# Attention with an MLP on one core: a hand-written opening, and q and k turned on VectorE from the seventh group on

## The chip, the cores and the metric

The kernel runs on one core of a Trainium2 chip. The metric is the device time of one execution in microseconds, lower is better; a run's time is that of its slowest core, and here there is only one.

## The reference

q, k and v have the shape (8, 12, 448, 64) in float32: 8 batches, 12 heads, 448 tokens, 64 features a head. Each row of q and k is normalised by its root mean square and multiplied by a gain; then comes attention, then a two-layer MLP over all 3584 tokens with 768 features, 2048 hidden units, and a slope alpha for each hidden unit where the hidden value is negative.

```python
def rmsnorm(x, g):
    rms = np.sqrt(np.mean(x * x, axis=-1, keepdims=True) + 1e-06)
    return x / rms * g
q_n, k_n = (rmsnorm(q, g_q), rmsnorm(k, g_k))
scores = scale * np.matmul(q_n, k_n.transpose(0, 1, 3, 2))
attn = softmax(scores)                      # written out in the reference
x = (attn @ v).transpose(0, 2, 1, 3).reshape(3584, 768)

h = x @ w_in                                # 768 x 2048
g = np.maximum(h, 0.0) + alpha * np.minimum(h, 0.0)
out = g @ w_out                             # 2048 x 768, float32
```

## The kernel before

**Groups, tiles, bursts.** The heads are taken in groups of four, three groups a batch, 24 groups in all, numbered y = 0 to 23 (`G = 3`, `NG = 24`). The 448 keys of a group are seven tiles of 64 (`J = 7`); a score tile is written (y, j). The whole run is a list of 69 bursts, written out by hand. A burst holds some score tiles, and behind them `gaps[n]`: steps of the MLP (`up`, `down` and, late in the run, the `quad` steps, which replace down steps by fewer products of mixed weights). Dictionaries say in which burst a group's factors are computed (`roots`), where its q and k are made ready (`turn_at`), where loads stand (`nexts`) and where softmax denominators and the product with v stand (`dens`, `avs`). `jobs[n]` holds small pieces that are put behind single steps of burst n, one after each `up`, and later in the run after every second one. The order of each engine's instructions is the order in which this code issues them.

**From q and k to their turned form.** For each group `load_qk` (L126) loads q and k in their natural layout, tokens on the partitions, by SP's queue. `square` (L177) squares them, mostly on GpSimd; `reduce` (L185, VectorE) sums the squares; `root` (L195, L196, ScalarE) takes the power -1/2 by Ln and Exp; `scale` (L205) multiplies q and k by it into the f16 tile `qs`, for the first groups on VectorE, later on GpSimd. Then q and k are turned, so that features lie on the partitions. For the first seven groups, `TD = 7`, TensorE does it: 14 transposes (L330) into PSUM, which VectorE evicts to `qT` (L337) and `kT` (L339, with the gain). From y = 7 on, `turn_dma` (L304) issues two DMA transposes on SP's queue right behind the scale, and some bursts later `turn` multiplies k by the gain in place on VectorE (L315, in the form that also writes an accumulator):

```python
if y >= TD:
    t = qkT[y, "k"].rearrange("p j g c -> p (j g c)")
    nc.vector.tensor_scalar(
        out=t, in0=t, scalar1=gain[:, 0:1], scalar2=None, op0=ALU.mult,
        op1=ALU.max, accum_out=mark32,
    )
```

**Attention and MLP.** `score` (L357, TensorE) makes a score tile in PSUM (tag "sc", two tiles of two banks) and `soft` (L371, ScalarE) takes its exponential to `expT`. `den` and `attv` (L382, TensorE) sum over keys, with ones and with v; `log` and `invert` (ScalarE) give the reciprocal, and VectorE writes x of the batch (L464, L481). An `up` step is six products of `w_in` and x into a bank `hT` of tag "mm" (L496; some use a spare bank, `hTa`); ScalarE writes the part scaled by alpha (L536), and VectorE combines both into `gT` (L540), which frees the bank. `down` (L558) multiplies by `w_out`, VectorE evicts (L569), and SP's queue stores (L546). The quads add products (L623), sums on VectorE and GpSimd (L611, L612, L619), mixed weights on GpSimd (L591), and evictions with sums (L681, L686).

**The opening.** The first eleven bursts (0 to 10) go through the same loop, with special cases: q and k of group 0 are taken in parts (`part_square` L171, `part_reduce`, `part_root`, `part_scale` L245, `part_turn` L256, `part_copy` L266 and L272), group 1 is turned by `turn_one`, and one burst, `lead`, has an order of its own. The gains and alpha come by GpSimd loads into one tile, which one transpose turns to columns (L995). `spin` issues products without a use, which keep TensorE busy. `follow` (L279) is a one-column copy on GpSimd that makes its queue wait for a scale.

Of the kernel before, what the change touches and what calls it, by code (L numbers as in the profile page):

```python
# [21 lines left out]
def kernel(  # L22
# [26 lines left out]
    TD = min(7, NG)  # L49
# [31 lines left out]
    cols = cst.tile([128, NF + 2], FP32, name="cols", tag="cols")  # L81
    alpha_sb = cols[:, :NF]
# [24 lines left out]
    SRC = {"q": q4, "k": k4}  # L107


    rows = lent(0, 512)[: NF + 2]  # L110

    def load_qk(y, hold=False):
        b, i = divmod(y, G)
        for nm in "qk":
            if y in (2, 5, 8):
                t = lent(HB + "qk".index(nm) * NB4, NB4).rearrange(
                    "p (h j d) -> p h j d", h=2, j=J
                )
            else:
                t = ld.tile([128, 2, J, D], FP32, name="nat", tag="nat", bufs=4)  # L120
            if hold and nm == "q":

                nc.scalar.copy(out=t[:, 0, 0, 0:1], in_=expb)
            o = t.rearrange("p h j d -> p h (j d)")
            for h in range(2) if (y, nm) == (0, "q") else (slice(0, 2),):
                nc.sync.dma_start(out=o[:, h], in_=SRC[nm][b, :, ds(2 * i, 2)][:, h])  # L126
            nat[y, nm] = t
# [9 lines left out]
    def load_w_in(c):  # L137

        src = moe_w_in[:512].rearrange("(n x p) f -> n p x f", n=4, p=32)
        for n in range(4):  # L140
            nc.gpsimd.dma_start(
                out=w_in_sb[ds(32 * n, 32), :4, ts(c, FB)], in_=src[n, :, :, ts(c, FB)]
            )
        if c % 2 == 0:
# [18 lines left out]
    def square(y, nm):  # L163
# [6 lines left out]
        if (y, nm) == (1, "q"):  # L170
            nc.scalar.activation(out=sqf, in_=src, func=AF.Square)  # L171
        else:

            n = 2 if (y, nm) in ((2, "q"), (G, "k")) else 1
            for h in range(n):
                c = ts(h, 2 * J * D // n)
                nc.gpsimd.tensor_mul(out=sqf[:, c], in0=src[:, c], in1=src[:, c])  # L177
# [20 lines left out]
    def scale(y, nm):  # L198
        if y in (1, 3, 5):
            t = lent(HB + 4 * NB4 + "qk".index(nm) * NB4 // 2, NB4 // 2).bitcast(FP16)  # L200
            t = t.rearrange("p (j h d) -> p j h d", j=J, h=2)
        else:
            t = ld.tile([128, J, 2, D], FP16, name="qs", tag="qs", bufs=2)
        eng = nc.vector if y < G or (y, nm) == (G, "q") else nc.gpsimd
        eng.tensor_mul(  # L205
            out=t.rearrange("p j h d -> p h j d"),
            in0=nat[y, nm],
            in1=rr_t[y][:, "qk".index(nm)].unsqueeze(3).broadcast_to((128, 2, J, D)),
# [33 lines left out]
    def part_scale(nm, j, n, eng):  # L242
        if (0, nm) not in qs:
            qs[0, nm] = ld.tile([128, J, 2, D], FP16, name="qs", tag="qs", bufs=2)
        eng.tensor_mul(  # L245
            out=qs[0, nm][:, j].rearrange("p j h d -> p h j d"),
            in0=nat[0, nm][:, :, j],
            in1=rr_t[0][:, "qk".index(nm), :, j].unsqueeze(3).broadcast_to((128, 2, n, D)),
# [11 lines left out]
    def part_copy(nm, j, eng):  # L260
# [4 lines left out]
        if nm == "k":  # L265
            nc.vector.tensor_scalar(  # L266
                out=o, in0=tp, scalar1=gain[:, 0:1], scalar2=None, op0=ALU.mult
            )
        elif eng is nc.scalar:
            nc.scalar.copy(out=o, in_=tp)  # L270
        else:
            eng.tensor_copy(out=o, in_=tp)  # L272
# [4 lines left out]
    def follow(y, nm):  # L277

        nc.gpsimd.tensor_copy(out=mark, in_=qs[y, nm][:, J - 1, 1, D - 1 : D])  # L279

    def turn_one(y, nm):
        t = psf.tile([128, 512], FP32, name="tps", tag="mm")
        tp = t[:, :S].bitcast(FP16).rearrange("p (j c) -> p j c", j=J)
        for j in range(J):
# [3 lines left out]
        t = att.tile([128, J, 2, 64], FP16, name=f"{nm}T", tag=f"{nm}T", bufs=3)  # L288
        o = t.rearrange("p j g c -> p j (g c)")
        if nm == "q":  # L290
            nc.vector.tensor_copy(out=o, in_=tp)
        else:

            for c in (slice(0, 2), slice(2, J)):
                nc.vector.tensor_scalar(
                    out=o[:, c], in0=tp[:, c], scalar1=gain[:, 0:1], scalar2=None,
                    op0=ALU.mult,
                )
        qkT[y, nm] = t

    def turn_dma(y):
        for nm in "qk":
            t = att.tile([128, J, 2, 64], FP16, name=f"{nm}T", tag=f"{nm}T", bufs=3)
            nc.sync.dma_start(  # L304
                out=t.rearrange("p j g c -> p j (g c)"),
                in_=qs[y, nm].rearrange("p j h d -> p (j h d)"),
                transpose=True,
            )
            qkT[y, nm] = t

    def turn(y):

        if y >= TD:
            t = qkT[y, "k"].rearrange("p j g c -> p (j g c)")
# [5 lines left out]
        if y <= G:  # L320
            ps = [psf.tile([128, 512], FP32, name="tps", tag="mm") for _ in "qk"]
        else:
            ps2 = psa.tile([128, 2, 512], FP32, name="tps2", tag="acc")
# [26 lines left out]
    def score(y, j):  # L350
        qT, kT = qkT[y, "q"], qkT[y, "k"]
        sc = pss.tile([128, 2, 512], FP32, name="sc", tag="sc")
        m = 64 if y < EARLY else 32
        for c in range(64 // m):
            for par in range(2):
                for g in range(2):
# [4 lines left out]
                        lhsT=kT[ds(64 * par, 64), j, g, ts(c, m)],  # L361
                        rhs=qT[ds(64 * par, 64), :, g, :],
# [13 lines left out]
    def over_keys(accs, ys, weights):  # L376

        heads = [(y, par, c) for y in ys for c in range(3 - len(ys)) for par in range(2)]
        for j in range(J):
# [17 lines left out]
    def ones_over(accs, ys):  # L397

        if not halved(ys):
            return over_keys(accs, ys, lambda g, y, par, c, j: ones[ds(64 * g, 64)])  # L400
# [13 lines left out]
    def den(ys):  # L414
        dn = psa.tile([128, 2, 512], FP32, name="dn", tag="acc")
        ones_over((dn[:, 0], dn[:, 1]), ys)
        rden[ys] = dn
# [23 lines left out]
    def attv(ys, half, spare=False, jobs=(), put=None, early=False):  # L441

        b, i = divmod(ys[0], G)
# [5 lines left out]

        if half:  # L450
            av, accs = None, [psf.tile([128, 512], FP32, name="avb", tag="mm") for _ in range(2)]
        else:
            pool, tag = (pss, "sc") if spare else (psa, "acc")
            av = pool.tile([128, 2, 512], FP32, name="av", tag=tag)
            accs = (av[:, 0], av[:, 1])
        over_keys(accs, ys, weights)
        for f in jobs:
            f(ys)
        if b not in xT:
            xT[b] = att.tile([128, 2, G, S], FP16, name="xT", tag="xT")  # L460
# [31 lines left out]
    def up_part(hT, b, ft, lo, hi):  # L492

        for i in range(lo, hi):
            for g in range(2):
# [4 lines left out]
                    start=(i == 0 and g == 0),  # L500
                    stop=(i == G - 1 and g == 1),
                )

    def begin(ft):

        if ft < 2:
            begun[ft] = bank("hT", False)
        elif ft == 2:
            t = psa.tile([128, 2, 512], FP32, name="hTb", tag="acc")
            begun[2], begun[3] = t[:, 0], t[:, 1]  # L510
        up_part(begun[ft], 0, ft, 0, G - 1)
# [3 lines left out]
    def up(b, ft, spare=False):  # L515
        if b == 0 and ft in begun:
            hT = begun[ft]

            for n in {2: (2, 3), 3: ()}.get(ft, (ft,)):
                up_part(begun[n], 0, n, G - 1, G)  # L520
        else:
            hT = bank("hT", spare)
            up_part(hT, b, ft, 0, G)
# [300 lines left out]
    turn_at[2], turn_at[G] = 5, av_at[0]  # L824
    turn_at.update(
# [157 lines left out]
    nc.gpsimd.dma_start(out=rows[:NF], in_=moe_alpha.rearrange("(t p) -> t p", p=128))  # L983
    for n, g in enumerate((g_q, g_k)):
        for h in range(2):
            nc.gpsimd.dma_start(
                out=rows[NF + n : NF + n + 1, ds(64 * h, 64)], in_=g.unsqueeze(0)
            )
    load_qk(1, True)
    load_qk(2)  # L990

    spin(2)
    spin(17, False)
    ct = psf.tile([128, 512], FP32, name="ct", tag="mm")
    nc.tensor.transpose(ct[:, : NF + 2], rows, ident32[: NF + 2, : NF + 2])  # L995
    K0 = 3
    both, full, lo, hi = slice(0, 2), slice(0, J), slice(0, K0), slice(K0, J)
    for h in range(2):
        part_square("q", slice(h, h + 1), full, nc.scalar)
    for h in range(2):  # L1000
        part_reduce("q", slice(h, h + 1), full)
    part_root("q", full)
    part_scale("q", full, J, nc.gpsimd)
    part_square("k", both, lo, nc.scalar)
    part_square("k", both, hi, nc.scalar)
    part_reduce("k", both, lo)
    part_reduce("k", both, hi)
    part_root("k", lo)
    part_scale("k", lo, K0, nc.vector)
    part_root("k", hi)  # L1010
    square(1, "q")
    nc.vector.tensor_copy(out=cols, in_=ct[:, : NF + 2])
    nc.vector.tensor_mul(
        out=gain, in0=cols[:, NF : NF + 1], in1=cols[:, NF + 1 : NF + 2]
    )
# [3 lines left out]
    part_copy("k", lo, nc.vector)  # L1019
    load_v(0)  # L1020
    part_scale("k", hi, J - K0, nc.vector)
    follow(0, "k")
    square(1, "k")
    reduce(1, "q")
    square(2, "q")
    after(0, part_turn, "k", range(K0, J))
    after(0, part_copy, "k", hi, nc.vector)
    after(0, reduce, 1, "k")
    after(0, reduce, 2, "q", (0,))
    mid[1] = 1  # L1030
    after(1, square, 2, "k")
    after(1, load_w_in, 0)
    after(3, reduce, 2, "q", (1,))
    after(3, reduce, 2, "k")
    after(5, load_w_in, 1)
    after(7, load_w_in, 2)
    after(8, load_w_in, 3)
    for c in range(4):
        after(first + (0, 0, 3, 4)[c], load_w_out, c)
    for nm in "qk":  # L1040
        after(first, square, 2 * G, nm)
    mid[4] = 2

    since = 2
    for n in range(NB):
# [4 lines left out]
        lead = n == den_at[G - 1]  # L1050
        first_tiles = tiles[: 2 if lead else split.get(n, 2)]
        for t in first_tiles:
            if t == (0, J - 2):
                spin(1)
            elif t == (1, J - 3):
                spin(2, False)
            elif t == (1, J - 2):
                spin(1, False)
            elif t == (0, J - 1):
                turn_one(1, "q")  # L1060
            elif t == (1, 0):
                turn_one(1, "k")
# [167 lines left out]
```

## Time and profile before

| | |
|---|---|
| median of three runs | 413.3 us (412.49, 413.3, 414.25) |
| the profiled execution, its own time | 414.78 us |
| its span in the profile | 413.0 us |
| mean granted TensorE clock | 0.995 |
| TensorE busy | 398.9 us, 97% |
| VectorE, ScalarE, GpSimd busy | 65%, 62%, 62% |
| data moved | 53.38 MB, 129 GB/s on the mean |

The span runs from the first to the last instruction of the profiled execution; the device time lies 1.8 us above it. "PE" is TensorE's products, "PEld" its loads of weights, "DVE" is VectorE, "ACT" ScalarE, "POOL" GpSimd, "SP" the engine that issues most DMAs. A row of groups tells line, engine, operation, output and input tile, shape, count; then busy time, mean duration in ns; then the idle time of the engine ahead of them and what ended it. A row of the timeline tells start, duration and instruction, with the idle time ahead of it in brackets.

### The profile page before, as it was taken

How to read it: one execution, taken by the hardware profiler on the slowest of the kernel's cores; microseconds unless marked ns; L12 is line 12 of the kernel's file. 1: busy time of each engine (PE TensorE's matmuls, PEld its weight loads, DVE VectorE, ACT ScalarE, POOL GpSimd, SP SyncE). 2: the span in 40 equal slices, each digit the busy share in tenths (PEclk: the TensorE clock that was granted, in tenths of full speed). 3: DMA queues.
4: the chain of work that ended last, by engine and by line, in shares of the span. 5: the costliest groups of instructions: out<-in, count | busy, mean ns of one | idle time of the engine just before them, and what ended most of it. 6: DMA issues, size and time to landing. Idle time of an engine off the chain costs nothing.

```text
span 413.0 us, 11724 instructions
## 1 busy us (share of the span) xinstructions
PE 398.9 (97%) x5055; PEld 208.1 (50%) x5055; DVE 266.9 (65%) x420; ACT 257.3 (62%) x390; POOL 255.8 (62%) x184
## 2 busy tenths in 40 slices
PE   7889999899999999999999999999999999999996
PEld 3344445444456445554455445545555455645664
DVE  3876875476567388785688585958576755465322
ACT  5697787567846785557766786875657783135110
POOL 5599996589677969376373847484724407300870
PEclk9899999999999999999999999999999999999999
DMA  8999899957754894329861697279332700320143
GB/s 259 231 217 206 172 200 155 248 169 103 163 81 134 204 169 91 115 63 197 144 168 48 173 138 177 63 180 193 59 75 54 127 3 24 75 59 0 30 103 97
DMA packets 67330, 53.38 MB, mean 129 GB/s; under 512 B 34880, under 2 KB 66768, under 8 KB 67280
## 3 DMA queue, kind: packets, MB, share of 16 engines
q1 hardware_dynamic: 53344, 40.45, 40.5%
q0 software_dynamic: 13536, 11.81, 21.5%
q8 instruction: 39, 0.64, 0.7%
q10 hardware_dynamic: 400, 0.39, 0.3%
q14 instruction: 11, 0.09, 0.1%
HBM read 45.62 MB, written 11.01 MB: 137 GB/s over the span
## 4 chain that ended last, share of the span: by engine, by line
PE 49%; DVE 6%; ACT 0%; issue 0%; DVEq 0%
PE hT L496 14%; PE hTa L496 7%; PE qx L623 5%; PE sc L357 3%; PE oq L623 3%; PE qc L623 3%; PE qz L623 2%; PE av L382 2%; PE oqm L623 2%; PE avb L382 1%; PE dn L382 1%; PE oqa L623 1%; DVE ss L185 1%; DVE xT L481 1%; DVE kT L315 1%; PE qza L623 1%
## 5 line engine op out<-in xcount | busy, mean ns | idle before, releaser
L371 ACT ACTIVATE expT<-sc 128x896 f16<-128x896 f32 x168 | 147.8, 913 | 55.4 <-PE sc L357 55.0
L496 PE MATMUL hT<-xT,w_in_sb 128*128 128x448 f16 x546 | 113.7, 353 | 0.4 <-DVE gT L540 0.2
L496 PEld LDWEIGHTS <-w_in_sb 128*128 128x128 f16 x768 | 72.7, 98 | 74.8 <-issue 10.1
L540 DVE TENSOR_TENSOR gT<-hT,gT 128x448 f16<-128x448 f32 x91 | 56.6, 623 | 40.1 <-ACT gT L536 39.2
L205 POOL TENSOR_TENSOR qs<-nat,rr 128x896 f16<-128x896 f32 x36 | 60.9, 1713 | 33.4 <-issue 24.9
L536 ACT ACTIVATE gT<-hT,cols 128x448 f16<-128x448 f32 x90 | 56.9, 633 | 33.9 <-PE hT L496 33.7
L177 POOL TENSOR_TENSOR sq<-nat 128x896 f32<-128x896 f32 x32 | 53.1, 1681 | 38.0 <-DMA nat<-in_q_dram 25.3
L357 PE MATMUL sc<-qT,kT 64*32 64x448 f16 (+1 forms) x1092 | 53.3, 358 | 3.5 <-ACT expT L371 1.1
L623 PEld LDWEIGHTS <-gT 128*128 128x128 f16 x352 | 33.4, 98 | 26.0 <-issue 4.9
L496 PE MATMUL hTa<-xT,w_in_sb 128*128 128x448 f16 x210 | 45.4, 352 | 0.0
L185 DVE TENSOR_REDUCE ss<-sq 128x14 f32<-128x896 f32 (+1 forms) x37 | 38.3, 1052 | 0.6 <-POOL sq L177 0.6
L481 DVE TENSOR_TENSOR xT<-av,rden 64x448 f16<-64x448 f32 (+1 forms) x37 | 27.2, 734 | 13.5 <-PE av L382 5.5
L536 ACT ACTIVATE gT<-hTa,cols 128x448 f16<-128x448 f32 x35 | 22.2, 635 | 19.1 <-PE hTa L496 19.1
L540 DVE TENSOR_TENSOR gT<-hTa,gT 128x448 f16<-128x448 f32 x35 | 21.8, 624 | 17.7 <-ACT gT L536 17.6
L357 PEld LDWEIGHTS <-kT 64*32 64x32 f16 (+1 forms) x1092 | 15.6, 93 | 34.7 <-issue 29.3
L558 PE MATMUL op<-w_out_sb,gT 128*128 128x384 f16 x160 | 27.4, 326 | 0.0
L382 PEld LDWEIGHTS <-vt 64*32 64x32 f16 x1344 | 20.2, 92 | 14.1 <-issue 5.0
L611 POOL TENSOR_TENSOR gs<-gT 128x1024 f16<-128x1024 f16 x3 | 6.4, 2121 | 30.3 <-DVE gT L540 28.1
L558 PEld LDWEIGHTS <-gT 128*128 128x128 f16 x192 | 18.0, 98 | 13.5 <-issue 2.4
L382 PE MATMUL av<-expT,vt 64*32 64x448 f16 x896 | 24.3, 350 | 0.3 <-DVE osb L671 0.3
L619 POOL TENSOR_TENSOR gT<-gT 128x1024 f16<-128x1024 f16 x11 | 23.8, 2166 | 0.0
L623 PE MATMUL qx<-w_out_sb,gT 128*128 128x384 f16 x120 | 20.9, 326 | 0.0
(148 smaller groups left out, 494.1 us busy)
## 6 DMA issues: line engine op xcount, KB each, us to landing
out_dram<-osb SPq DMA_DIRECT2D x107, 96.0 KB, 2.8
nat<-in_k_dram SPq DMA_DIRECT2D x21, 448.0 KB, 5.4
nat<-in_q_dram SPq DMA_DIRECT2D x20, 448.0 KB, 4.9
vt<-in_v_dram POOLq DMA_DIRECT2D x8, 672.0 KB, 11.0
w_in_sb<-in_moe_w_in_dram POOLq DMA_DIRECT2D x24, 128.0 KB, 5.0
w_out_sb<-in_moe_w_out_dram POOLq DMA_DIRECT2D x4, 768.0 KB, 10.8
arena<-in_q_dram SPq DMA_DIRECT2D x3, 448.0 KB, 7.8
arena<-in_k_dram SPq DMA_DIRECT2D x3, 448.0 KB, 8.5
```

The source lines that it names most:

```text
L177: nc.gpsimd.tensor_mul(out=sqf[:, c], in0=src[:, c], in1=src[:, c])
L185: nc.vector.tensor_reduce(out=o[:, c], in_=sqs[y, nm][:, c], axis=AXIS_X, op=ALU.add)
L205: eng.tensor_mul(out=t.rearrange("p j h d -> p h j d"), in0=nat[y, nm], in1=rr_t[y][:, "qk".index(nm)].unsqueeze(3).broadcast_to((128, 2, ...
L357: nc.tensor.matmul(out=sc[ds(64 * g + m * c, m), par, :S].rearrange("p (j c) -> p j c", j=J), lhsT=kT[ds(64 * par, 64), j, g, ts(c, m)], r ...
L371: nc.scalar.activation(out=expT[y][:, j], in_=scs[y, j][:, :, :S], func=AF.Exp, scale=QK_SCALE, bias=EXP_BIAS,)
L382: nc.tensor.matmul(out=accs[g][ds(32 * n, 32), :S], lhsT=weights(g, y, par, c, j), rhs=expT[y][ds(64 * g, 64), j, par, :], start=(j == 0), ...
L481: nc.vector.tensor_mul(out=x, in0=av, in1=r)
L496: nc.tensor.matmul(out=hT[:, :S], lhsT=w_in_sb[:, block_of(g, i), ts(ft, 128)], rhs=xT[b][:, g, i, :], start=(i == 0 and g == 0), stop=(i ...
L536: nc.scalar.activation(out=g, in_=hT[:, :S], func=AF.Copy, scale=alpha_sb[:, ft : ft + 1])
L540: nc.vector.tensor_max(out=g, in0=hT[:, :S], in1=g)
L558: nc.tensor.matmul(out=op[:, :OH], lhsT=gT[:, ft, ts(tile % J, 128)], rhs=w_out_sb[:, ft, ts(oh, OH)], start=(ft == 0), stop=(ft == NF - 1),)
L623: nc.tensor.matmul(out=bank[:, c], lhsT=g[:, ft], rhs=v[:, ft, c], start=(first and ft == 0), stop=(ft == HF - 1), skip_group_check=True,)
```

## The change

It has two parts.

The opening is written out. The loop begins at burst 11 (`first + 1`), and everything before it stands as a list of calls. In it k of group 0 is loaded in halves on ScalarE's queue beside q on SP's; the load of q of group 1 is held until the first half of q(0) is there; the two gains come by two SP loads and are multiplied before they are turned, and alpha is turned by itself, later; the squares of group 0 are all on ScalarE; q(0) is scaled on VectorE and part of k(0) on GpSimd; the turned first part of k(0) is copied by ScalarE; the loads of v and `w_in` are issued in pieces at other places; the sums over keys for groups 0 to 2 are split and placed between score tiles, and the first `up` steps are begun in thirds; group 3 is turned in a bank of tag "sc", behind the third part of x.

From y = 6 on (`TD = 6`: 18 groups, one more than before left TensorE) q and k are turned otherwise. They are loaded with 14 neighbouring rows of 64 values to a partition (`FLAT`, 3584 bytes in one piece instead of 1792). `scale` writes straight into `qT` and `kT`, the two halves of a partition's rows interleaved value by value. `flip` transposes 32 x 32 blocks of 32-bit words into a tile of `qs` on VectorE, copies it back on VectorE, and moves four quarter blocks of 32 partitions by DMA on SP's queue. The two flips of a group are jobs of the burst behind the one with its root. `turn` applies the gain at its place as before. `score` takes its operands by other indices, with unchanged products.

```diff
-    TD = min(7, NG)
+    TD = 2 * G
...
+            if y >= TD:
+                nc.sync.dma_start(
+                    out=t.rearrange("p h j d -> p (h j d)"), in_=FLAT[nm][b, i]
+                )
+                continue
...
+            for h in range(2) if y == 0 else (slice(0, 2),):
+                (nc.scalar if (y, nm) == (0, "k") else nc.sync).dma_start(
+                    out=o[:, h], in_=SRC[nm][b, :, ds(2 * i, 2)][:, h]
+                )
...
+        if y >= TD:
+            o = t.rearrange("p b j c -> p (b j c)").rearrange(
+                "p (j d h) -> p h j d", j=J, h=2
+            )
...
-    def turn_dma(y):
-        for nm in "qk":
-            t = att.tile([128, J, 2, 64], FP16, name=f"{nm}T", tag=f"{nm}T", bufs=3)
-            nc.sync.dma_start(
-                out=t.rearrange("p j g c -> p j (g c)"),
-                in_=qs[y, nm].rearrange("p j h d -> p (j h d)"),
-                transpose=True,
-            )
-            qkT[y, nm] = t
+    def flip(y, nm):
+
+        t = qkT[y, nm].rearrange("p b j c -> p (b j c)")
+        x = ld.tile([128, J, 2, D], FP16, name="qs", tag="qs", bufs=2).rearrange(
+            "p j h d -> p (j h d)"
+        )
+        nc.vector.transpose(
+            out=x.bitcast(FP32).rearrange("p (b j c) -> p j b c", b=2, j=J),
+            in_=t.bitcast(FP32).rearrange("p (j b c) -> p j b c", b=2, j=J),
+        )
+        nc.vector.tensor_copy(out=t, in_=x)
+        t, x = (a.rearrange("p (b c) -> p b c", b=2) for a in (t, x))
+        for par in range(2):
+            even, odd = ds(64 * par, 32), ds(64 * par + 32, 32)
+            nc.sync.dma_start(out=t[odd, 0], in_=x[even, 1])
+            nc.sync.dma_start(out=t[even, 1], in_=x[odd, 0])
...
-        if y <= G:
+        if y < G:
             ps = [psf.tile([128, 512], FP32, name="tps", tag="mm") for _ in "qk"]
         else:
-            ps2 = psa.tile([128, 2, 512], FP32, name="tps2", tag="acc")
+            ps2 = (
+                pss.tile([128, 2, 512], FP32, name="tps3", tag="sc") if y == G
+                else psa.tile([128, 2, 512], FP32, name="tps2", tag="acc")
+            )
...
-                        lhsT=kT[ds(64 * par, 64), j, g, ts(c, m)],
-                        rhs=qT[ds(64 * par, 64), :, g, :],
+                        lhsT=kT[ds(64 * par, 64), g, j, ts(c, m)],
+                        rhs=qT[ds(64 * par, 64), g],
...
             if y >= TD:
-                turn_dma(y)
+                jobs.setdefault(n + 1, []).extend((flip, (y, nm)) for nm in "qk")
```

The part of the opening that the prediction speaks of, from the first scales to the fourth group's turn:

```diff
+    for h in (one, two):
+        for nm in "qk":
+            part_square(nm, h, full, nc.scalar)
+            part_reduce(nm, h, full)
...
+    part_scale("q", full, J, nc.vector)
+    part_scale("k", lo, K0, nc.vector)
+    follow(0, "k", K0 - 1)
+    part_scale("k", hi, J - K0, nc.gpsimd)
...
+    part_copy("q", full, nc.vector)
+    part_copy("k", lo, nc.scalar)
...
+    follow(2, "k")
+    for y in (3, 4):
+        for nm in "qk":
+            square(y, nm)
...
+    load_w_in(1)
...
+    root(3)
+    scale(3, "q")
+    scale(3, "k")
+    load_w_in(2)
+    load_qk(6)
+    for nm in "qk":
+        square(5, nm)
...
+        nc.vector.tensor_mul(out=x[:, g, 2], in0=av[:, g, :S], in1=rden[third][:, g])
+    begin(2)
+    begin(3)
+    load_w_in(3)
+    up(0, 0)
+    turn(3)
+    up(0, 1)
+    up(0, 2)
+    tile_of(3, 0)
+    root(4)
+    for nm in "qk":
+        scale(4, nm)
...
-    for n in range(NB):
+    for n in range(first + 1, NB):
```

## The prediction

> **What bounds the kernel now.** I read part 1 of the page, then the windows by stage, then the costliest groups by form, and last the timeline where the change acts.
>
> ```profile
> PE 398.9 (97%) x5055; PEld 208.1 (50%) x5055; DVE 266.9 (65%) x420; ACT 257.3 (62%) x390; POOL 255.8 (62%) x184
> ```
>
> The windows (start:end, length, then busy time of PE, PEld, DVE, ACT, POOL, the clock, the DMA share, GB/s):
>
> ```profile
> 0.00:12.00 12.00, 8.37 (x40) 3.89 (x40) 5.16 (x13) 5.75 (x13) 6.11 (x15) 1.00 0.83 267
> 12.00:34.00 22.00, 19.68 (x306) 9.23 (x303) 17.61 (x25) 19.44 (x28) 19.07 (x25) 0.92 0.99 211
> 34.00:49.00 15.00, 14.38 (x200) 6.88 (x198) 10.41 (x15) 11.49 (x17) 14.99 (x18) 1.00 0.97 181
> 49.00:64.00 15.00, 14.84 (x118) 7.43 (x116) 11.01 (x18) 12.06 (x21) 14.95 (x12) 1.00 1.17 201
> 89.00:200.00 111.00, 110.46 (x1376) 56.68 (x1372) 76.36 (x118) 74.63 (x114) 82.34 (x51) 1.00 0.65 126
> 200.00:320.00 120.00, 118.45 (x1785) 62.07 (x1770) 87.22 (x138) 83.95 (x126) 69.47 (x41) 1.00 0.62 124
> ```
>
> From 89 to 320 us TensorE lacks 0.54 + 1.55 = 2.1 us in 231: nothing done on another engine there can gain more than that, except by taking work off TensorE. VectorE is busy 163.6 of the 231 (71%). In 34 to 64 us GpSimd has no time left (14.99 and 14.95 of 15). Only before 34 us does TensorE idle much, 3.6 + 2.3 us, and part of its busy time there is spins, which do no work.
>
> The groups by form (busy us, mean ns of one, idle before):
>
> ```profile
> L540 DVE TENSOR_TENSOR gT<-hT,gT 128x448 f16<-128x448 f32 x91 | 56.6, 623 | 40.1 <-ACT gT L536 39.2
> L337 DVE COPY qT<-tps 128x896 f16<-128x896 f16 x5 | 3.1, 621 | 0.7 <-PE tps L330 0.6
> L612 DVE TENSOR_TENSOR gs<-gs,gT 128x1024 f16<-128x1024 f16 x1 | 0.7, 691 | 0.0
> L612 DVE TENSOR_TENSOR arena<-arena,gT 128x1024 f16<-128x1024 f16 x7 | 7.6, 1083 | 0.4
> ```
>
> The same operation of L612 takes 691 ns once and 1083 ns on the mean of seven others. The timeline shows why:
>
> ```profile
> 206.13 3.78 POOL L205 TENSOR_TENSOR qs<-nat,rr 128x896 f16<-128x896 f32 x2
> 206.44 1.93 DVE L611 TENSOR_TENSOR arena<-gT 128x1024 f16<-128x1024 f16 x1
> 208.41 2.06 DVE L612 TENSOR_TENSOR arena<-arena,gT 128x1024 f16<-128x1024 f16 x1
> ...
> 212.52 0.76 PE L382 MATMUL avb<-expT,vt 64*32 64x448 f16 x24 [0.54 <-DVE osb L686]
> ```
>
> Beside GpSimd's scale each takes 1.93 to 2.06 us. VectorE is then 1.93 + 2.06 - 2 x 0.69 = 2.6 us late, and TensorE later waits 0.54 us for it. At 157 us the same pair (1.59 and 2.06, so 2.3 us late) costs TensorE nothing that the trace shows. So 4.9 us of lateness cost 0.54 us of TensorE: 0.11 per us, and at worst 0.21.
>
> **The opening.** By hand, with the rows' durations: half of k(0) is loaded on the other queue, its squares are on ScalarE, q's scale moves from GpSimd (1.69 us) to VectorE, and the gain no longer waits for four GpSimd loads. The first exponential starts at some 10.1 instead of 12.0 us. Tiles (1, 0) and (2, 6) come 3.8 and 2.7 us earlier, and x of batch 0 about 4 us earlier, but turn(3) and two tiles that lay ahead of it now follow it; tile (3, 3) is some 0.65 us earlier. Behind these stands GpSimd's chain, two squares each of y = 3 and 4 (3.35 each pair), w_in's issues (2.2 to 4.3), scales, squares of y = 5: its ready time for the scale of k(4) comes out at 46.9 to 48.1, against 48.4 before, where TensorE already waited:
>
> ```profile
> 45.06 3.35 POOL L205 TENSOR_TENSOR qs<-nat,rr 128x896 f16<-128x896 f32 x2
> ...
> 48.47 0.56 PE L330 MATMUL tps<-ident,qs 128*128 128x128 f16 x7 [0.54 <-POOL qs L205]
> ```
>
> So the opening is worth 0.3 to 1.8 us there if GpSimd's scale is what comes last, and up to 4 if later ups absorb that wait. I take -1.8, the better end of that chain, because everything ahead of it is 2.7 us and more earlier; bounds -0.3 and -4.
>
> **Group 6's turn.** Its 14 transposes leave TensorE, and two evictions (0.62 + 0.68) leave VectorE:
>
> ```profile
> 62.84 0.96 PE L330 MATMUL tps<-ident,qs 128*128 128x128 f16 x14
> ```
>
> TensorE is full there (14.84 of 15), so -0.95.
>
> **The flips.** 18 groups, so 36 tensors. Each adds on VectorE a block transpose of 448 32-bit words and a copy of 896 f16, and on SP's queue four moves of 28 KB; 34 DMA transposes go. No row shows a block transpose: the nearest, 448 words through VectorE in L540, is 0.62; above it stands 1.08 for a reduction over 896 words. The copy's nearest row, L337, takes 0.62 but reads PSUM; by L612's 0.69 for two inputs and 1024 columns, one input could be near 0.30. I take 0.62 + 0.45 = 1.07 a flip (bounds 0.92 and 1.7). 36 x 1.07 = 38.5 us. 32 of the 34 DMA transposes are issued between 89 and 320 us, so VectorE's load there goes from 163.6 to 197.8 of 231, 86%.
>
> On top comes GpSimd. It is busy 74 and 58% of the two long stages with pieces of about 1.7 us, so a copy that must stand behind one waits 0.66 x 0.85 = 0.56 on the mean. That a one-input copy waits at all no row shows: it may wait nothing (0), or a whole piece (1.7). The two-input rows above do, and GpSimd's work sits where the flips come, just behind the scale. I take 0.56. The Trainium skill ("SBUF — State Buffer", Who interferes with whom) speaks against the change here: a VectorE copy in its fast two-port form and a GpSimd operation exclude each other for the whole instruction, by order of issue, while the accumulating scale form and the reduction do not. By it copies placed inside a scale wait out the rest of it, up to 1.7 us. The trace agrees for the two-input forms (0.69 against 1.93 and 2.06), and for L315, the accumulating form, which keeps 1.13 to 1.14 us with GpSimd busy or idle; for a copy no run here shows it yet.
>
> A group's two flips then make VectorE 2 x (1.07 + 0.56) = 3.3 us late. Beside ups it wins back about 0.5 per up (up 1.13 on TensorE, 0.62 on VectorE), and by the timeline a bank is released about 1 us (median) ahead of its next use. Price: 3.3 x 0.11 = 0.36 us a group, 18 x 0.36 = 6.5. Bounds: nothing, if all is covered; and 3.3 less the 1.0 and two recoveries of 0.5, so 1.3 a group, 23 in all.
>
> **Waits and queues.** The gain on k (L315, unchanged at 1.13) now waits for moves instead of a DMA transpose. Eight issues at 0.37 to 0.58 are some 3.8 us of SP's queue a group, against 2.5 to 3.6 for two transposes; the 48 KB stores land after 2.0 us, the transposes after 2.9 to 3.7. The gain stands a burst or more later, so mostly nothing. The exception is y = 7, whose moves stand in SP's queue behind the loads of y = 9 and 10, which wait for buffers; VectorE's gains and evictions queue behind that gain. 0 to 2 us, I take 0.3. What is queued behind the flips on VectorE, the evictions of ups, is priced above. GpSimd's scale writes pairs with stride two: 1.71 a piece unless the stride costs; off the path after 64 us.
>
> **Sum** against the profiled 414.78 (span 413.0, 1.8 outside it): -1.8 - 0.95 + 6.5 + 0.3 = +4.05, so 418.8. The median shown, 413.3, lies 1.5 below the profiled run: 417.4.
>
> **Rivals.**
> (a) The flips are hidden: VectorE has 67 us free between 89 and 320, and 2.3 us of lateness at 157 cost nothing. Then 414.78 - 1.8 - 0.95 = 412.0, by the median 410.5, faster. It decides when a pair's lateness stays near 1.0 + 2 x 0.5 = 2 us, which means copies that do not wait for GpSimd (2 x 1.07). Against it: 212.52 above.
> (b) As (a), but the opening's full 4 us arrive: 408.3. For it: the DMA share is near 1 anyway and squares are earlier; against it, GpSimd without a gap from 34 to 64.
> (c) VectorE becomes the bound: copies meet scales nearly always and a transpose costs 1.1. At 1.3 us a group, 434; at three fifths of that price, 425. For it: 86% load and two operations in a row; against: waits recover in stretches of quads, where VectorE is less dense.
> (d) Flips cost 2 to 3 us and the opening returns them: 413, no change.
> That the change does not do what it says, the DMA transposes being the hidden limit that it removes, would show in TensorE waits on qT or kT; in 89 to 320 all its idle time is 2.1 us, so this adds little to (a).
>
> **How the numbers follow.** My forecast (415.4 to 422) 0.38, (a) 0.24, (b) 0.08, (c) 0.13, (d) 0.17. A measurement of this kernel can tell about 0.5%, 2.1 us. Faster is (a) and (b), 0.32; same is (d), 0.17; slower is the forecast and (c), 0.51. The range 408 to 427 reaches from (b) to the cheaper side of (c); the forecast's own range is 415.4 to 422.
>
> **What would show it.** Right: the copy's mean above 0.8 us with single ones near 2; L540's idle time falls, and TensorE gets waits on gT L540 of 0.2 to 0.4 us beside flips; busy TensorE about 397 but its idle time between 89 and 320 up by 5 or so. The first exponential near 10.1 and the scale of k(4) ready near 47. Wrong: copies at 0.3 to 0.5 beside GpSimd and no new TensorE waits, then (a); gains waiting for moves by more than 1 us, then the queue and not the lock is the cost; an opening that is more than 2 us ahead at down(0, 0), 63.6 before.

## The result, and the profile after

The changed kernel takes 475.38 us (median of 4 runs, 472.36 to 476.58); the kernel before takes 413.77 us beside it. The ratio is 1.148 (95% interval 1.141 to 1.154). The forecast was 417.4 us and a range of 408 to 427: slower as said, but by 61.6 us instead of 4.

Part 1 of the page of after (busy us, share of the span of 474.8 us, instructions):

```profile
PE 417.9 (88%) x5039; PEld 211.5 (45%) x5039; DVE 331.8 (70%) x492; ACT 258.4 (54%) x388; POOL 256.3 (54%) x178
```

Span less busy time is 56.9 us for TensorE, against 14.1 before: 42.8 us more idle time. The other 19.0 us of the longer span are busy time: fewer instructions, and yet 417.9 instead of 398.9 us. The granted clock accounts for it: 0.948 in this execution against 0.995 before, and 398.9 x 0.995 / 0.948 = 418.7. By stages, the windows of after (the last columns are clock, DMA share, GB/s):

```profile
34.00:64.00 30.00, 24.78 (x248) 11.29 (x232) 17.82 (x27) 19.64 (x33) 26.60 (x26) 0.94 0.96 178
89.00:200.00 111.00, 91.11 (x1031) 44.90 (x1032) 88.48 (x111) 59.10 (x90) 70.25 (x43) 0.94 0.36 92
200.00:320.00 120.00, 106.31 (x1594) 54.26 (x1593) 93.30 (x146) 72.65 (x108) 58.24 (x34) 0.94 0.37 96
```

The granted clock is 0.94 where it was 1.00, and TensorE idles 19.9 and 13.7 us in the two long stages that lacked 0.5 and 1.6 before. The groups by form, of after:

```profile
L538 PE MATMUL hT<-xT,w_in_sb 128*128 128x448 f16 x546 | 122.6, 370 | 17.5 <-DVE gT L583 17.1 <-DVE xT L1166 0.2
L332 DVE COPY kT<-qs 128x896 f16<-128x896 f16 x18 | 33.0, 1832 | 0.6
L332 DVE COPY qT<-qs 128x896 f16<-128x896 f16 x18 | 17.0, 944 | 0.8
L328 DVE STREAM_TRANSPOSE qs<-qT 128x448 f32<-128x448 f32 x18 | 11.5, 638 | 17.7 <-DMA qT<-qs 16.0 <-POOL qT L223 1.6
```

The ups on `hT` waited 0.2 us for VectorE before; now 17.1 (first row above). The row of before:

```profile
L496 PE MATMUL hT<-xT,w_in_sb 128*128 128x448 f16 x546 | 113.7, 353 | 0.4 <-DVE gT L540 0.2
```

The copies take 50.0 us in all, 36 times 1.39. The transposes take 0.64 each, and those of q wait 16.0 us for moves (those of k another 2.0). Two stretches of the timeline show the two kinds of stall. First a copy that waits for GpSimd, called the lock from here on:

```profile
107.63 0.88 POOL L142 DMA_DIRECT2D vt<-in_v_dram  x1
107.80 7.51 DVE L332 COPY kT<-qs 128x896 f16<-128x896 f16 x1
108.53 1.65 POOL L634 TENSOR_TENSOR arena<-w_out_sb,arena 128x768 f16<-128x768 f16 x1
110.14 1.69 POOL L223 TENSOR_TENSOR qT<-nat,rr 128x896 f16<-128x896 f32 x1
111.78 1.68 POOL L223 TENSOR_TENSOR kT<-nat,rr 128x896 f16<-128x896 f32 x1
113.43 1.62 POOL L634 TENSOR_TENSOR arena<-w_out_sb,arena 128x768 f16<-128x768 f16 x1
115.23 0.61 DVE L583 TENSOR_TENSOR gT<-hT,gT 128x448 f16<-128x448 f32 x1
115.89 2.40 PE L538 MATMUL hT<-xT,w_in_sb 128*128 128x448 f16 x6 [6.12 <-DVE gT L583]
122.77 1.31 PE L538 MATMUL hT<-xT,w_in_sb 128*128 128x448 f16 x6
```

A copy that takes 0.39 us when GpSimd is idle ends only after four GpSimd operations in a row. The eviction behind it frees its bank late, and TensorE stands for 6.12 us. Then its next six products take 2.40 us, and only from 122.8 on 1.31 again: in the trace the granted clock is 0.50 from 114.9 to 121.8. The run has six such stretches of 6.8 us, and each begins in one of the six gaps of TensorE above 3 us; the gap of 2.25 us has none behind it. Second, the moves:

```profile
223.26 0.39 DVE L332 COPY kT<-qs 128x896 f16<-128x896 f16 x1
225.93 0.58 SPq L337 DMA_DIRECT2D qT<-qs  x1
232.91 0.65 DVE L328 STREAM_TRANSPOSE qs<-qT 128x448 f32<-128x448 f32 x1 [6.92 <-DMA qT<-qs]
234.57 1.65 PE L538 MATMUL hTa<-xT,w_in_sb 128*128 128x448 f16 x4 [6.50 <-DVE gT L583]
```

Here no copy waits. A move of 28 KB, issued at 225.93, is landed 6.9 us later; the next group's transpose needs the `qs` buffer that this move reads, and the evictions stand behind the transpose. (The last row counts four products, because the view ends at 236.)

### The profile page after: what moved, and what is told of

Its sections match the earlier page's. It is cut to its first block, busy times and chain, and to the rows that moved or that the text cites. A ratio compares the mean times of both kernels' runs of the same rounds, so it can differ in the third digit from the quotient of the medians.

```text
span 474.8 us, 11968 instructions
## 1 busy us (share of the span) xinstructions
PE 417.9 (88%) x5039; PEld 211.5 (45%) x5039; DVE 331.8 (70%) x492; ACT 258.4 (54%) x388; POOL 256.3 (54%) x178
## 4 chain that ended last, share of the span: by engine, by line
PE 28%; DVE 9%; issue 8%; DMA 4%; POOL 3%; SPq 2%; ACT 0%; DVEq 0%; POOLq 0%; ACTq 0%
PE hT L538 7%; PE hTa L538 4%; PE qx L666 3%; PE oq L666 3%; DMA qT<-qs 3%; PE qc L666 2%; PE oqm L666 2%; PE qz L666 1%; DVE xT L523 1%; DVE qs L328 1%; PE sc L391 1%; PE oqa L666 1%; POOL qT L223 1%; DVE ss L192 1%; DVE kT L343 1%
## 5 line engine op out<-in xcount | busy, mean ns | idle before, releaser
L538 PE MATMUL hT<-xT,w_in_sb 128*128 128x448 f16 x546 | 122.6, 370 | 17.5 <-DVE gT L583 17.1
L538 PEld LDWEIGHTS <-w_in_sb 128*128 128x128 f16 x768 | 75.4, 101 | 108.9 <-issue 50.1
L184 POOL TENSOR_TENSOR sq<-nat 128x896 f32<-128x896 f32 x32 | 53.8, 1695 | 65.7 <-DVE ss L192 65.4
L538 PE MATMUL hTa<-xT,w_in_sb 128*128 128x448 f16 x210 | 48.0, 367 | 7.6 <-DVE gT L583 7.5
L223 POOL TENSOR_TENSOR qT<-nat,rr 128x896 f16<-128x896 f32 x17 | 29.2, 1719 | 40.6 <-ACT rr L203 40.5
L192 DVE TENSOR_REDUCE ss<-sq 128x14 f32<-128x896 f32 x36 | 38.1, 1077 | 0.0
L332 DVE COPY kT<-qs 128x896 f16<-128x896 f16 x18 | 33.0, 1832 | 0.6
L523 DVE TENSOR_TENSOR xT<-av,rden 64x448 f16<-64x448 f32 (+1 forms) x35 | 25.0, 714 | 7.8 <-ACT expT L405 3.4
L601 PE MATMUL op<-w_out_sb,gT 128*128 128x384 f16 x160 | 29.9, 346 | 0.0
L666 PE MATMUL qx<-w_out_sb,gT 128*128 128x384 f16 x120 | 23.5, 353 | 6.9 <-DVE gT L583 5.1
L223 POOL TENSOR_TENSOR kT<-nat,rr 128x896 f16<-128x896 f32 x17 | 29.4, 1727 | 0.0
```

Of the source, the lines that this page charges most:

```text
L184: nc.gpsimd.tensor_mul(out=sqf, in0=src, in1=src)
L192: nc.vector.tensor_reduce(out=o[:, c], in_=sqs[y, nm][:, c], axis=AXIS_X, op=ALU.add)
L223: eng.tensor_mul(out=o, in0=nat[y, nm][:, :, js], in1=rr_t[y][:, "qk".index(nm), :, js].unsqueeze(3).broadcast_to((128, 2, js.stop - js.st ...
L332: nc.vector.tensor_copy(out=t, in_=x)
L538: nc.tensor.matmul(out=hT[:, :S], lhsT=w_in_sb[:, block_of(g, i), ts(ft, 128)], rhs=xT[b][:, g, i, :], start=(start and k == 0 and g == 0) ...
L601: nc.tensor.matmul(out=op[:, :OH], lhsT=gT[:, ft, ts(tile % J, 128)], rhs=w_out_sb[:, ft, ts(oh, OH)], start=(ft == 0), stop=(ft == NF - 1),)
```

## Experiments

The theory after the first look: the loss is the lock, the moves and the halved clock that follows long idle times. The rivals: VectorE has too much work whatever it waits for; or the opening loses.

**The two parts apart (e1, e2).** e1 takes the changed opening with the turning of before, e2 the opening of before with the flips. The cut shows the lines that switch; the loads, scales and turns that belong to them go along:

```diff
# e1, in the changed kernel
-    TD = 2 * G
+    TD = min(7, NG)
-                jobs.setdefault(n + 1, []).extend((flip, (y, nm)) for nm in "qk")
+                turn_dma(y)
# e2, in the kernel before
-    TD = min(7, NG)
+    TD = 2 * G
-                turn_dma(y)
+                jobs.setdefault(n + 1, []).extend((flip, (y, nm)) for nm in "qk")
```

> The changed opening with the turning of before (TD = 7, DMA transposes). Theory: the opening itself loses, because GpSimd's chain (second scale of k(3) beside VectorE's, w_in issued behind it, squares of y = 5 ahead of the scale of k(4)) makes k(4) ready at 52.6 instead of 48.4 us; the first down starts near 71 instead of 63.6 us and the time is 419 to 422 us. Rival: the lateness at 50 to 72 us comes from the flips of group 6 and the other loads; then the first down starts near 62 and the time is 410 to 413 us.

> The opening of before with the flips from y = 6 on. Theory (the flips carry most of the loss, by copies that wait for trains of GpSimd work, and by the lower clock that follows the idle time): 455 to 468 us, granted clock 0.94 to 0.96, some copies of 3 us and more. Rival (the two parts cost only together): under 430 us.

e1: 416.67 us, ratio 1.008 (1.005 to 1.011). e2: 463.19 us, ratio 1.121 (1.113 to 1.129). The opening costs 3.3 us and the flips 49.9 (each above the kernel before beside it), so the flips carry the loss, as the theory of e2 had it. The two add up to 53, the whole is 61.6. The profiled executions of the whole and of e2 differ by 10.6 us: the whole has 5.7 us more in gaps of TensorE above 2 us and 6.7 us more TensorE busy time. Why the stalls are longer there was not settled. e1 came out 2 to 5 us below the expectation; its first down starts at 68.5, against 63.6 before and 71.9 in the whole.

**The copy without the lock (e3, e4).**

```diff
-        nc.vector.tensor_copy(out=t, in_=x)
+        nc.vector.tensor_scalar(          # e3
+            out=t, in0=x, scalar1=1.0, scalar2=None, op0=ALU.mult,
+            op1=ALU.max, accum_out=mark32,
+        )
+        nc.scalar.copy(out=t, in_=x)      # e4, in its place
```

> The changed kernel with the copy of the flip as a scale by one that also writes an accumulator, the form of the gain. Theory (waiting for GpSimd's lock is the loss): each copy takes 1.13 to 1.15 us, none more; idle time of TensorE behind gT falls from 30 us to under 10; granted clock back to 0.98; 430 to 442 us, the rest being the opening and the waits for moves. Rival (VectorE has simply too much work): the copies' floor rises from 0.39 to 1.14, so 27 us more of plain VectorE work and 470 us or more. Rival (the moves' landing is the loss): 465 to 476 us.

> The changed kernel with the flip's copy on ScalarE. Theory (lock): copies of about 0.9 us on ScalarE, no lock; VectorE has only the 0.64 us transposes more; 428 to 440 us. Rival (moves land late): 465 us or more, transposes still waiting 16 us for qT<-qs.

e3: 466.55 us, e4: 477.93 us. Both miss their theory (430 to 442 and 428 to 440) and lie where the rival of the late moves had put them. In e3 every copy takes 1.09 us and none more, so the lock is gone, but the time falls by 9 us only. The waits of e3 (engine and line, releaser, us in all, times, longest):

```profile
DVE qs L328 <- DMA qT<-qs: 19.5, 3, 7.0
DVE qs L328 <- DMA kT<-qs: 8.2, 2, 6.6
```

VectorE's transposes wait 27.7 us for moves, against 18.0 in the changed kernel, and its gains 6.9 against 1.1. One wait took the other's place. In e4 the copies take 0.94 us on ScalarE, whose own evictions now stand behind the transposes (52.7 us of waits for L328), and the transposes' wait for moves is there too (19.3 us).

**What delays copies and moves (e5, e6, e7).** The 7.5 us copies begin while GpSimd issues the load of v, and 22 of the 26 moves that take 4.5 us or more are on their way while v's 672 KB are.

```diff
# e5, and e6 with e3's copy
-        after(av_at[G * b - 1] + 1, load_v, b)
+        after(av_at[G * b - 1] + 3, load_v, b)
# e7, with e3's copy
-        name="qs", tag="qs", bufs=2
+        name="qs", tag="qs", bufs=4
-        name="osb", tag="osb", bufs=6
+        name="osb", tag="osb", bufs=4
```

> The changed kernel with the loads of v for batches 2 to 7 issued two bursts later, away from the flips of the same places. Theory (GpSimd issues v just ahead of a flip; from then on the copy waits for a train of GpSimd work, and the moves stand behind v's 672 KB): the copies of 4.3 to 7.5 us and the waits of 5 to 7 us for moves go, TensorE keeps its full clock, 430 to 450 us. Rival (the train is GpSimd's own work and the moves stand behind the loads of q and k): 465 to 476 us, with the same long waits.

> As the run with the late loads of v, and with the copy in the accumulating form that never waits for GpSimd. Theory (two waits, one behind the other: the lock, then the moves that stand behind v): 425 to 440 us, no gap of TensorE above 3 us. Rival (moves stand behind the loads of q and k, whatever v does): 455 to 467 us, waits of the transposes for qT<-qs of 15 us in all or more.

> The accumulating copy, and four buffers qs instead of two (osb has four instead of six to make room), so that a group's transposes do not wait for the moves of the group before. Theory (late moves hurt only through the buffers): waits of the transposes for moves vanish, no gap above 3 us, 425 to 440 us; the wait shows up in the gains instead if moves land more than 10 us late. Rival (VectorE has too much work, waits are incidental): 455 us or more.

e5: 459.51 us, e6: 455.06, e7: 448.04. e5 and e7 lie between theory and rival, e6 at the rival's edge, so v's place and the buffers are each a part of it and neither is all. In e5 the four copies above 3 us are gone; one of 8.36 us has come, which starts 0.01 us after an issue of v. The moves land after 1.9 instead of 2.4 us (median), and one in ten still after 5.0 or more (5.9 before that edit). In e7 the transposes no longer wait for moves, and the wait turns up where the expectation put it, at the gain (6.9 us in e3):

```profile
DVE kT L346 <- DMA kT<-qs: 17.9, 6, 5.0
```

**Neither, and each alone (e9, e10, e11).** e9 and e10 leave out the moves, with e3's copy and with the plain one, so the off-diagonal blocks of q and k stay where they were and the scores are not the reference's; e11 is whole: e3's copy, e7's buffers and e5's loads.

```diff
-            nc.sync.dma_start(out=t[odd, 0], in_=x[even, 1])
-            nc.sync.dma_start(out=t[even, 1], in_=x[odd, 0])
```

> The accumulating copy, and the four moves of each flip are left out (so q and k keep their off-diagonal blocks where they were, and the scores are not the reference's). Theory (waits for the moves, through buffers and gains, are what is left once the lock is gone): no gap of TensorE above 2 us between 90 and 400 us, full clock, 425 to 436 us. Rival (VectorE's plain work is the bound): within 10 us of the 448 us with four buffers.

> The changed kernel with its plain copy, and the moves left out as in the run beside it. What it takes above that run is the lock alone: theory 12 to 25 us more, with copies of 4 to 7 us where GpSimd has just issued the load of v. Rival (the lock costs only where moves wait too): no more than that run, since a copy's floor is 0.39 instead of 1.08 us.

> Accumulating copy, four buffers, and v issued two bursts later: the computation is whole. Theory (moves wait behind v, and gains behind moves): the gains' waits of 18 us fall below 8 and the time to 432 to 442 us. Rival (moves wait behind q's and k's loads and behind each other): 444 to 450 us.

e9: 436.89 us, e10: 458.49, e11: 441.92. e9 falls between its theory (up to 436) and its rival (438 and more), e10 and e11 into their theories, e11 at the edge: its gains still wait 8.8 us for moves. These runs separate the parts. With moves and lock both gone, 23.1 us above the kernel before are left. The plain copy takes 21.6 us more than the lock-free one, although its floor is 0.39 against 1.09. So 21.6 is what the lock costs more than the slower form; what it costs against a copy of 0.39 us that never waits, no run shows. The copies of e9, then of e10:

```profile
L332 DVE TENSOR_SCALAR_CACHE_REDUCE kT<-qs 128x896 f16<-128x896 f16 x18 | 19.5, 1086 | 0.6
```

```profile
L332 DVE COPY kT<-qs 128x896 f16<-128x896 f16 x18 | 37.4, 2079 | 0.6
```

The moves cost 475.38 - 458.49 = 16.9 us with the plain copy and 466.55 - 436.89 = 29.7 us with the lock-free one: where the lock already stalls, moves can land under the stall; that is a reading of the two differences, not tested by itself. e11, with buffers and a later v, comes to 5.0 us above e9.

**The opening, and a faster kernel (e8, e12, e16).** All three have no flips. They reorder GpSimd's work ahead of the turn of group 4.

```diff
# e8: the lines with + come behind the scales of group 4
-    for nm in "qk":
-        square(5, nm)
...
-    load_w_in(3)
...
     for nm in "qk":
         scale(4, nm)
+    load_w_in(3)
+    for nm in "qk":
+        square(5, nm)
# e16: as e8, but the square of q(5) stays ahead, and behind the scales come
+    square(5, "k")
+    load_w_in(3)
# e12: as e16, with the DMA transposes of y = 6 one burst later, and
-    TD = min(7, NG)
+    TD = 2 * G
```

In all three the reduction of q(5) moves into the next burst.

> The changed opening with the turning of before; the squares of y = 5 and the last load of w_in go behind the scale of k(4) on GpSimd. Theory (the opening loses at GpSimd's chain ahead of k(4)): the scale of k(4) ends near 48 instead of 53 us, the first down starts near 64 to 66, and the time is 411 to 414 us. Rival (loads and the clock hold the opening, not GpSimd's order): 416 to 418 us as without it.

> The changed opening with squares of q(5) ahead of, and of k(5) behind, the scale of group 4, w_in's last load behind that, and DMA transposes from y = 6 on (TD = 6) as before from 7 on; no flips. Theory (GpSimd's order is what holds the opening, and the 14 transposes of group 6 cost TensorE 0.95 us): first down near 63 us, 410 to 413 us, up to 0.8% below the kernel before. Rival (other waits take its place): 414 to 417 us.

> The changed opening with the turning of before (TD = 7), the square of q(5) ahead of the scale of group 4 on GpSimd, that of k(5) and w_in's last load behind it. Theory (GpSimd's order ahead of turn(4) held the opening back): 411.5 to 413.5 us, 0.2 to 0.6% below the kernel before. Rival (other waits in the opening take its place): 414 to 417 us.

e8: 416.17 us, ratio 1.005 (1.001 to 1.009). e16: 415.26, 1.005 (1.003 to 1.007). e12: 420.68, 1.015 (1.010 to 1.020). None beats the kernel before; e8 and e16 come out at their rivals, e12 above both of its ranges. In e8 the scale of k(4) ends at 45.7 and in e16 at 48.2 us, 5 to 8 us earlier than in e1 (53.3), but the first down starts at 65.7 and 66.5, only 2 to 3 us earlier. In e8 VectorE's reduction of y = 5 then waits 2.1 us for the square that was put back. So GpSimd's order is a part of it, not the whole; what holds the rest was not settled. In e12 the harm shows in one wait of VectorE's gain for the DMA transpose of k(6), which is issued at 66.5 us and waited for until 81.0, where the DMA share is 1.31 to 1.56 (64 to 89 us; 1.05 in the kernel before):

```profile
DVE kT L323 <- DMA kT<-qs: 9.3, 1, 9.3
```

**What the plain work costs (e13, e14, e15, e17, e18).** e13 leaves out the flips, e14 their copies and moves; none of the five moves anything, and so none has the reference's scores; e15 is e9 with k's flip one burst later (but for y = 7), e17 is e10 with the late v, e18 is e9 with half of the columns copied.

```diff
# e13
-                jobs.setdefault(n + 1, []).extend((flip, (y, nm)) for nm in "qk")
# e18
-            out=t, in0=x, scalar1=1.0,
+            out=t[:, : J * D], in0=x[:, : J * D], scalar1=1.0,
```

> The changed kernel with the flips left out whole (transposes, copies, moves), so q and k go into the scores unturned. Theory (the 20 us that are left without lock and moves are VectorE's plain work): 414 to 418 us, as the opening alone, less 0.95 us of TensorE. Rival (the flat loads, GpSimd's strided scale or the opening's late end cost them): 425 us or more.

> As the changed kernel with copies and moves left out: only the 36 transposes of 0.64 us stay. Theory (VectorE's lateness costs above a slack of some 1 us per group): 1.3 us a group beside ups, so 2 to 7 us above the run without flips. Rival (each us on VectorE costs its share from the first on, 20 us per 62 us of work): 7 to 8 us above it. Rival (the lock takes the transposes too): 15 us or more above it, with transposes of over 1 us.

> As the run with accumulating copies and no moves (436.9 us), with k's flip one burst behind q's instead of right behind it (y = 7 unchanged). Theory (two flips of 1.72 us close together use up the slack of the banks): 4 to 12 us less. Rival (all that counts is VectorE's sum of work): 435 to 438 us.

> The changed kernel with its plain copy, no moves (458.5 us), and the loads of v for batches 2 to 7 two bursts later. Theory (the lock's price sits in the few copies of 4 to 7.5 us that start while GpSimd issues v): those copies go, at most one stays, no gap of TensorE above 3 us in those places, 436 to 447 us. Rival (the price sits in the many copies of 0.5 to 2 us): 452 to 460 us.

> As the run with accumulating copies and no moves (436.9 us), with only half of the columns copied (half of each tile stays unturned), so a flip is some 1.2 us of VectorE instead of 1.72. Theory (VectorE's slack in the bursts of ups carries the transposes' 0.64 us for 1 us in all and then is used up): 420 to 428 us. Rival (a fixed price of the second instruction of a flip, whatever its length): 433 to 438 us.

e13: 415.48 us, ratio 1.006 (1.004 to 1.009), so the flat loads and the strided scale cost nothing that shows above the opening's own loss (3.3 us in e1). Set in order of the time that VectorE spends on flips (transposes and copies, from each run's rows by form), with no moves in any of them:

| run | VectorE's time on flips, us | time above the kernel before, us | us per us since the row above |
|---|---|---|---|
| e13, no flips | 0 | 2.5 | |
| e14, transposes | 22.8 | 3.5 | 0.04 |
| e18, half the copy | 45.2 | 9.0 | 0.25 |
| e9, lock-free copy | 62.0 | 23.1 | 0.84 |
| e17, plain copy, v late | 69.8 | 36.0 | 1.65 |
| e10, plain copy | 78.6 | 44.7 | 0.99 |

The price is near nothing for the first third and about one to one or above at the end. Each single rate is rough. By the intervals of e13 and e14 the first one can be anything up to about 0.13. The reads of the accumulator, 3.0 us each in e18 and e9, are not in the second column; with them the rates from e14 to e18, from e18 to e9 and from e9 to e17 are 0.22, 0.84 and 2.7. And the last two rows are of another kind: there VectorE stands in a few long waits, behind which TensorE's gaps grow and its clock falls (0.981 and 0.970, against 0.991 in e9). e13 and e18 came out inside their theories, e14 below even its own (2 to 7 us above e13). Of the runs with flips and without long stalls the least and the most loaded, part 1 of the page, e14 and then e9:

```profile
PE 398.9 (96%) x5039; PEld 207.3 (50%) x5039; DVE 282.5 (68%) x456; ACT 257.5 (62%) x388; POOL 254.1 (61%) x178
```

```profile
PE 403.4 (93%) x5039; PEld 208.2 (48%) x5039; DVE 319.6 (73%) x528; ACT 258.0 (59%) x388; POOL 254.3 (58%) x178
```

VectorE's mean share moves only from 68 to 73%, which hides it. Cut into pieces of 6 us, from 90 us to some 35 to 39 us before the end, VectorE is busy over 95% in 2 of 48 pieces before, 5 of 48 in e14, 13 of 49 in e18, 15 of 51 in e9: the flips fall in bursts of ups, where reductions, gains and evictions already are. e9's added idle time is many waits of TensorE below 2 us for VectorE, no long one. e15 (440.28 us, above both of its ranges) speaks against the narrower reading that two flips close together are the matter: spread over two bursts they cost no less. e17 (448.96) lies between its theory and its rival: v's later place is worth 9.5 of the 21.6 us. A copy of 8.36 us that starts behind an issue of v is still in it, with a gap of TensorE of 8.7 us, so the share of these few copies is not settled.

## Why the prediction was right or wrong

- **Direction and mechanism: right.** TensorE has the bound, the flips make VectorE late, and copies wait for GpSimd. The Trainium skill ("SBUF — State Buffer", Who interferes with whom) says that of a VectorE copy in its two-port form and a GpSimd instruction the second to issue is blocked for the whole instruction. The trace agrees that the plain copy is blocked and the accumulating form is not (1.09 us each, e3), and differs in length: waits of up to four GpSimd instructions in the changed kernel.
- **The opening: wrong in sign.** -1.8 forecast, and -0.95 for group 6; +2.5 to +3.3 measured (e13, e1). The first exponential does start early, at 10.09. The step that failed first is the time for GpSimd's chain, 46.9 to 48.1. The timeline of after:

```profile
36.08 2.60 POOL L223 TENSOR_TENSOR arena<-nat,rr 128x896 f16<-128x896 f32 x1 [2.94 <-ACT rr L203]
49.29 3.34 POOL L223 TENSOR_TENSOR qs<-nat,rr 128x896 f16<-128x896 f32 x2
52.69 0.56 PE L361 MATMUL tps<-ident,qs 128*128 128x128 f16 x7 [1.07 <-POOL qs L223]
```

  The scale of k(3) waits 2.9 us for ScalarE's root and takes 2.60 beside VectorE's scale instead of 1.70; later it waits 0.85 us more for a load of `w_in`. All that GpSimd does afterwards shifts, and k(4) is ready 4.2 us later than before, not up to 1.5 earlier. A second step failed with it, that this time decides what the opening is worth: e8 and e16 have k(4) ready at 45.7 and 48.2 and still lose 1.7 and 2.2 us.
- **The size of the flips' work: too small.** 0.62 + 0.45 + 0.56 = 1.63 us a flip forecast; 0.64 + 1.39 = 2.03 measured, a quarter more. The copy alone takes 0.39, so its wait is 1.00 on the mean instead of 0.56, and the largest is 7.1 where the forecast allowed one piece of 1.7.
- **The price of that lateness: the step that failed most.** 0.11 us of TensorE per us, from two stretches of quads and a single delay each. Only the first third of the load is as cheap (0.04 in e14); all 73 us of it would have cost 8 us at that price, and by interpolation in the table cost some 37. TensorE's idle time between 89 and 320 us is up by 31.5 us, not by 5 or so. The upper bound that I worked out (1.3 us a group, 23 in all) is by chance near the 23.1 of e9, which has no lock and no moves and the opening's loss in it. Rival (c), VectorE as the bound, has the price right, but not its condition: 24 of 36 copies wait, not nearly all, and a transpose takes 0.64, not 1.1; it got 13%, and its 425 to 434 us were too low as well.
- **The moves: wrong.** 0.3 forecast, for one gain; 17 measured, although the gains themselves wait 1.1 us in all. Moved work was looked at by who waits for its result, not by who waits for its buffers: the next group's transpose writes the `qs` buffer that a move still reads.
- **The clock: left out.** 19 us of the 61.6 are busy time of TensorE. It came with the long gaps: in the changed kernel 7 gaps above 2 us hold 32.4 us and the mean granted clock is 0.948; in e9 there is none, the clock is 0.991 and TensorE is busy 403.4 us. The Trainium skill ("TensorE: Matmul & The Clock Gate", Part 1: The HAM clock gate) says that an idle window of about 3.4 us halves the clock until one busy window has passed. The trace agrees in kind: ahead of the row at 115.89 the granted clock falls to 0.50 some 5.2 us into the gap, and stays there for 6.8 us.

In sum, above the kernel before and added in this order: everything but the flips 2.5, transposes 1.0, copies with their lock 41.2 (a form of 1.09 us without the lock costs 19.6 in their place), moves 16.9; together 61.6. In another order the shares differ: with the lock-free copy the moves cost 29.7.

## What to carry to other kernels

The price of making a busy helper engine later is no constant: here it was near zero until the local slack was used, and then about one to one; a price taken from one small delay must not be multiplied by fifteen times that delay. Look at the engine's load in pieces of a few us where the new work would land, not at its mean share. When a transfer takes over part of a step, ask also who needs the buffers it reads, and expect that removing one wait uncovers the next.

## What the hardware showed unexpectedly

A blocked VectorE copy does not always get its turn at the next boundary between GpSimd instructions. All 16 copies above 3 us in five runs (the changed kernel, e2, e5, e10, e17) began while GpSimd issued a DMA, or at most 0.5 us after that issue, and then waited through two to five GpSimd instructions, 3.1 to 8.4 us. Of the 108 others above 0.5 us, with no such issue ahead, 104 waited for the end of one GpSimd operation and were done 0.24 to 0.26 us behind it. Two of 1.92 us began less than 0.05 us before such an end and waited through the next operation too, and two of 2.0 us waited through the DMA issue behind theirs. Five that began inside an issue took 0.39 us at once; why is not shown. A block transpose of 448 32-bit words a partition never waited for GpSimd: 0.63 to 0.65 us each in the changed kernel.
